# Attention, Fourier mix and feed-forward in one kernel: every buffer of a group named singly, and batch 0's sums in two equal parts

## The chip, the core and the metric

The kernel runs on one core of one Trainium2 chip (trn2). The core has a matrix engine (TensorE, "PE" in the profile; its weight loads are shown apart as "PEld"), VectorE ("DVE"), ScalarE ("ACT"), GpSimd ("POOL") and SyncE ("SP"), each with its own queue of instructions that run in the order in which they were written. Data lie in SBUF, matmul results in PSUM, which is split into eight banks. DMA transfers are issued by an engine's queue ("SPq", "POOLq", "ACTq") and run beside it.

The metric is the time on the device in microseconds (us), from runs of the whole kernel. The profile comes from one further execution.

## The reference

Inputs are q, k and v of shape (4, 8, 768, 64) (batch, heads, sequence, head dimension), and two weights of 512 x 2048 and 2048 x 512. All are fp32, as is the output of 4 x 768 x 512. Cut to what matters:

```python
scores = scale * q @ k.T                     # per batch and head, 768 x 768
keep   = (key < 8) | (0 <= query - key < 96) # 8 global keys, 96 local ones
scores = where(keep, scores - slope[h] * dist, -1e9)
a      = exp(scores - max); a = a / (sum(a) + 1e-9)
x      = concat_heads(a @ v)                 # 4 x 768 x 512
u      = x + real(fft(fft(x, axis=1), axis=2))
un     = (u - mean(u)) / sqrt(var(u) + 1e-6)
out    = u + relu(un @ w_ch1) @ w_ch2
```

## The kernel before

**Tiling.** Matmuls take fp16. The sequence has six blocks of 128 rows, the model dimension four of 128, the hidden layer sixteen. Heads go in pairs, so that a batch has four pairs, and pair n = 4b + hp carries its number through the names: `v_5` is the v of batch 1, pair 1. Attention computes only the band around the diagonal and the eight global keys. For a pair there are a cast of q and k to fp16, their transposes `qkT`, three score tiles `sc_n_g`, each followed by an exp on ACT (`ex`), and, once all pairs of a part are there, `pav` (probabilities times v), which VectorE divides by the row sums to give `x` (L762 reciprocal, L763 product; together "the norm"). In batches 0 and 1 the rows of v are also rearranged by matmuls with an identity (`v_place`: POOL casts the landed v at L437, the matmuls `pvp_n` follow at L453).

The Fourier mix of a batch starts with sums and differences of x on VectorE (`fold_s`, L810 to L829, then `fold_d`, L904 to L921), goes on with `py` matmuls (transform over the sequence, four groups), whose results ACT and DVE move to SBUF, and `pu` matmuls (over the model dimension; three pairs of row residues for each batch, so 12 units c = 3b + pr). An addition on VectorE (L1046, L1055) adds x back. For this addition x is needed with its rows in another order: the kernel writes x to DRAM (`xd`, L782, two halves of the columns for batch 0) and reads it back as `xr` (L790). Then come the statistics (`sm`, L1067), the scaling `un` (L1077, L1079, L1086), its transposes `ptu` and `unT`, the first feed-forward matmul `ph` in eight units for each c (L1144, relu at L1150 on ACT or L1151 on DVE) and the second, `pg` (L1167; for c of 8 and above the form of `pgA` and `pgD` at L1248, which takes seven products of sums of blocks for eight), and the store of `u` to the output.

**Order.** The order of all instructions is made while the kernel is built, by the class `Plan`. It is a list scheduler: it keeps a clock `t` per engine, a dictionary `tok` of the times at which results are there, a list of work that is ready for DVE, ACT, POOL and SP (`later`, `emit`), and four streams of matmul units (`run`): MIX and ATT, in which it may look ten units ahead, and PH and PG, which go in order. At each step it takes the unit that can start first by its own clocks. Costs are formulas (`act`, `dve`, `pool`, `mm_us`), and the landings of the early DMAs are a table written by hand:

```python
LAND = {("xw", 0, 0): 34.0, ("xw", 0, 1): 36.0, ("xr", 0): 41.0,
        ("ld", 4, 2): 47.7, ("ld", 5, 2): 53.4, ("ld", 6, 2): 58.9, ("ld", 7, 2): 64.7, ... }
```

Here `("ld", 4, 2)` is the landing of v_4, `xw` the write of x and `xr` its read. What the planner decides is only the order in each queue; the waits on the chip are those that the data, the buffers and the DMA semaphores need. The v loads of batch 1 (L388) are issued by SP and come behind the read of xr by an explicit token (`("xi",)`). The weights are eight DMAs of POOL (L1395, L1400), the loads of batches 2 and 3 wait behind a small DMA that needs the last weight (L1409, `hold`).

**Buffers.** The planner counts the free buffers of a group itself. In PSUM, group `xx` has two slots of two banks each, and `C` and `D` are two more such slots in the early part; their banks go later to `ph` and `pg`, two slots of one bank each. `rings` holds for each group a list of the times at which a slot comes free; `slot` takes the first of the list, whichever of the physical slots that was, and `bank` asks the pool for the next tile of the group's tag, which the pool hands out in rotation. In SBUF, `buf(tag, i, ...)` asks for buffer i of a group with `bufs=NBUF[tag]`, again handed out in rotation; the planner makes the user of number i wait for the token `("free", tag, i - NBUF[tag])`. Groups with more than one buffer are `hT` 3, `qk` 2, `qs` 3, `qkT` 4, `er` 2, `v0` 2, `u` 4, `un` 2 and `unT` 2.

**Sums of batch 0.** `fold_s` splits batch 0's columns in three parts, 0 to 256, 256 to 384 and 384 to 512. Each part is ten VectorE instructions (`f1` to `f4`) and waits for the x of its own columns; batch 0's norms come in the order of pairs 0 and 1 together, pair 2, pair 3. The folds of batch 0 have rank -1 in the planner, so that it lets them go up to 0.8 us ahead of other work. The parts have numbers of their own in the groups `eA` and `ww` (functions `IA`, `NA`, `IW`).

Of the kernel before, what the change touches and what calls it, by code (L numbers as in the profile page):

```python
# [9 lines left out]
FP16 = mybir.dt.float16  # L10
# [2 lines left out]
ALU = mybir.AluOpType  # L13

P = 128


class Plan:
# [73 lines left out]
    def emit(self, place):  # L92
        ready, (_, ways, needs, after, outs, uses, ring, lat, dma, then, _, nd) = self.ready.pop(place)
        if nd:
            ready = [max(r, self.lanes[nd - 1]) for r in ready]
        ends = [max(self.t[w[0]], r) + w[1] for w, r in zip(ways, ready)]
        i = int(np.argmin(ends))
        eng, _, fn = ways[i]
        fn()
        end = self.t[eng] = ends[i]  # L100
        if dma:
            q = "DMA2" if outs and outs[0][0] in ("xw", "xr") and outs[0][1] == 0 else "DMA"
            end = self.t[q] = max(self.t[q], end) + dma
        else:
            lat += self.LAT.get(eng, 0.0)
        for o in outs:
            self.tok[o] = max(end + lat, self.LAND.get(o, 0.0)) if dma else (end + lat, eng)
        for u in uses:
            self.used(u, end + lat)
        for _ in range(nd):  # L110
            self.lanes.append(max(end + lat, self.t[eng] + 2.2, *[self.LAND.get(o, 0.0) for o in outs]))
            self.lanes.pop(0)
        if ring is not None:
            self.rings[ring].append(end + lat)
        if then is not None:
            then(end + lat)
        self.promote()
# [8 lines left out]
        return end + 0.15  # L126

    def slot(self, tag):
        return self.rings[tag].pop(0)

    LOOK = 10
    AHEAD = 0.8
# [1 line left out]
    def run(self, streams):  # L134

        left = [list(s) for s, _ in streams]
        while True:
            best = None
            for i, s in enumerate(left):
                for k, (needs, ring, _) in enumerate(s[:self.LOOK if streams[i][1] else 1]):  # L140
                    if not self.known(needs):
                        continue
                    r = self.at(needs, "PE")
                    if ring is not None:

                        there = [(self.rings[g][0], g) for g in ring
                                 if self.rings[g] and not (g in ("C", "D") and ("CD",) in self.tok)]
                        if not there:
                            continue
                        t, g = min(there)  # L150
                        r = max(r, t + self.SEM)
                    else:
                        g = None
                    c = (max(r, self.t["PE"]), i, k, g or "")
                    if best is None or c < best:
                        best = c
            op = self.first()
            if op is not None and (best is None or op[0] <= best[0]):
                self.emit(op[4])
            elif best is not None:  # L160
                needs, ring, fn = left[best[1]].pop(best[2])
                if ring is not None:
                    self.slot(best[3])
                fn(best[0], best[3])
# [29 lines left out]
def kernel(  # L194
# [82 lines left out]

    pl = Plan()
    RING = {"xx": 2, "ph": 2, "pg": 2}
    pl.rings = {r: [0.0] * n for r, n in RING.items()}  # L280

    pl.rings["C"] = [0.0]
    pl.rings["D"] = [0.0]
# [4 lines left out]
    def bank(tag, name, dtype=FP32):  # L288
        if tag in ("C", "D"):
            return early["pool"].tile([P, 2, 512 if dtype == FP32 else 1024], dtype, tag=tag, name=name, bufs=1)  # L290
        if tag == "xx":
            return ps.tile([P, 2, 512 if dtype == FP32 else 1024], dtype, tag=tag, name=name, bufs=RING[tag])
        if "late" not in early:
            early["ctx"].__exit__(None, None, None)
            early["late"] = ctx.enter_context(tc.tile_pool(name="psl", bufs=1, space=bass.MemoryType.PSUM))
        return early["late"].tile([P, 512], FP32, tag=tag, name=name, bufs=RING[tag])


    NBUF = {"hT": 3, "qk": 2, "qs": 3, "qkT": 4, "er": 2, "v0": 2, "eg": 1, "x": 1, "xr": 1, "zy": 1, "eA": 1,
# [5 lines left out]

    def buf(tag, i, shape, dtype, users):
        pl.users(("free", tag, i), users)
        return wk.tile(shape, dtype, tag=tag, name=f"{tag}_{i}", bufs=NBUF[tag])

    ident = kon.tile([P, 256], FP16, tag="ident", name="ident")  # L310
    sel_sb = ident[:, 128:256]
# [129 lines left out]
    def v_place(b, hp):  # L441
        n = HP * b + hp

        def run(start, ring):
# [17 lines left out]
            def freed(t):  # L462
                done.append(t)
                if len(done) == 2:
                    pl.rings[ring].append(max(done))
                    for x in CD(b, ring):
                        pl.used(x, max(done))
            for a in range(2):
# [80 lines left out]
    def trans(b, hp):  # L549
        if b >= FB:  # L550
            return trans_dma(b, hp)
        n = HP * b + hp

        def run(start, ring):
            pt = bank("xx", f"pt_{n}", FP16)
# [161 lines left out]
    def av(b, part, jp):  # L717
# [8 lines left out]
        def run(start, ring):  # L726
# [30 lines left out]

            def norm():
                if b not in X:
                    X[b] = buf(XT[b][0], XT[b][1], [P, NS, Dm], FP16, 4 if b else 5)  # L760
                rc = wk.tile([P, 2, nh, 1], FP32, tag="rc", name=f"rc_{b}_{first}_{jp}", bufs=2)
                V.reciprocal(rc, pv[:, :, :, 64:65])  # L762
                VT(X[b][:, 2 * jp:2 * jp + 2, first * Dh:(first + nh) * Dh].rearrange("p j (h d) -> p j h d", d=Dh),  # L763
# [88 lines left out]
    def fold_3(b):  # L852

# [280 lines left out]
    def ph_unit(c, jp):  # L1134
        needs = [("unT", c), ("w1", jp // 2)] + (free("hT", 4 + c) if jp == 0 else []) + [("CD",)]

        def run(start, ring):
            if jp == 0:
                HT[c] = buf("hT", 4 + c, [P, NJ, CH], FP16, 2 if c < CS else 1)
            ph = bank("ph", f"ph_{c}_{jp}")  # L1140
            for a in range(2):
                jb = 2 * jp + a
                for d in range(ND):
# [13 lines left out]
    def pg_unit(c, t, part):  # L1157
# [3 lines left out]

        def run(start, ring):
            if part == 0:
                GP[0] = bank("pg", f"pg_{c}_{t}")
            pg = GP[0]
            for jb in range(4 * part, 4 * part + 4):
                nc.tensor.matmul(pg, HT[c][:, jb, t * P:(t + 1) * P], W2[0][:, jb, :],  # L1167
# [10 lines left out]
            pl.later([("DVE", dve(512), add)], [("rstd", c)], e, [("ob", i)], ring="pg", rank=0)  # L1178
# [62 lines left out]
    def pg_units(c):  # L1241
# [24 lines left out]
            V.scalar_tensor_tensor(o, x, r(t), acc, op0=ALU.mult, op1=ALU.add)  # L1266

        def p1(start, ring):
            A_ = GP[c, "A"] = bank("pg", f"pgA_{c}")
            prod(A_[:, 0:HC], a(0, 0), bw(0, 0), True)  # L1270
            e = pl.pe(one_us, start)
            pl.later([("DVE", dve(HC), lambda: stt(u(0)[:, 0:HC], A_[:, 0:HC], 0, u(0)[:, 0:HC]))],
                     [("rstd", c)], e, [("ra", c, 0)], rank=0)

        def p45(start, ring):
            D_ = GP[c, "D"] = bank("pg", f"pgD_{c}")
# [15 lines left out]
        def p32(start, ring):  # L1292
# [3 lines left out]
            e = pl.pe(2 * one_us, start)  # L1296
            pl.used(("free", "sx", 3 * (c - CS) + 2), e)
            pl.later([("DVE", dve(Dm), lambda: stt(u(0), D_, 0, u(0)))],
                     [("ra", c, 1)], e, [("ob", c, 0)], ring="pg", rank=0)

        def p7(start, ring):
            A_ = GP[c, "A"]
# [7 lines left out]
            pl.later([("DVE", dve(Dm), last)], [("rd", c, 0)], e, [("ob", c, 1)], ring="pg", rank=0)  # L1310

        h0 = [("h", c, jp) for jp in range(4)]
        h1 = [("h", c, jp) for jp in range(4, 8)]
# [15 lines left out]
    with tc.manual_schedule():  # L1329
# [9 lines left out]
            load(0, hp, "v")  # L1339

        V.memset(EG, 0.0)
        pz = bank("xx", "pz")
# [25 lines left out]

        def ones(start, ring):

            pv = bank("xx", "pones")
# [153 lines left out]
```

## Time and profile before

| what | value |
|---|---|
| time, median of 5 runs | 270.75 us (270.43 to 272.6) |
| time of the profiled execution | 270.43 us |
| its span, first to last instruction | 268.2 us |
| mean granted TensorE clock | 0.985 |
| matmuls `ph` (L1144) | 768, busy 94.3 us |
| matmuls `pg` (L1167) | 256, busy 60.2 us |
| matmuls `pav` (L743) | 352, busy 17.3 us |
| exps of scores on ACT (L629, L632) | 24 and 24, 0.94 and 0.93 us each |
| relu on ACT (L1150) / DVE (L1151) | 78 of 0.60 us / 18 of 0.69 us |
| loads of v (L388, of all batches) | 16 DMAs of 192 KB, 4.6 us from issue to landing |
| weight loads on POOL's queue | 8 DMAs of 512 KB, 17.1 us from issue to landing |

The first row is what a user of the kernel sees; the profile explains only the execution in the second row, and 2.2 us of it lie outside the span. Busy time is a sum over the whole span, and the mean of one instruction can mix shapes. The last two rows are medians of the time from the issue, most of which a transfer can spend waiting behind others. The page of the profile also gives the busy share of each engine in 40 slices of 6.7 us; TensorE and the granted clock (tenths of full speed) read:

```profile
PE   7898889689999999999999999999999999999993
PEclk9999799979999999999999999999999999999999
```

The low digit in the eighth slice (47 to 54 us) and the low clock in the ninth (54 to 60 us) lie in one stretch of the kernel, in which batch 1's attention and batch 0's Fourier mix run together. The clock is also low in the fifth slice (27 to 34 us).

### The profile page before, as it was taken

To read this page: it belongs to the slowest core of one execution; us is meant where nothing else is said; L and a number is where in the kernel's file an instruction comes from. 1 tells how busy PE (TensorE), PEld (TensorE's weight loads), DVE (VectorE), ACT (ScalarE), POOL (GpSimd) and SP (SyncE) were. 2 spreads that over 40 slices of the span, in tenths; PEclk is the share of its full clock that TensorE was granted. 3 is DMA by queue.
4 is the path that set the end of the run, shared out by engine and by line. 5 is a ranking of instruction groups with operands and counts; after the bars stand their busy time and mean duration, and the time that the engine had idled before them with its cause. 6 is when DMAs were issued, how large, how long until landed. Compare 5 with 4: busy or idle time off the path is not lost.

```text
span 268.2 us, 6166 instructions
## 1 busy us (share of the span) xinstructions
PE 254.0 (95%) x2512; PEld 181.7 (68%) x2512; DVE 175.8 (66%) x375; ACT 146.1 (54%) x244; POOL 67.3 (25%) x131
## 2 busy tenths in 40 slices
PE   7898889689999999999999999999999999999993
PEld 3444745468784696778776466778865678888882
DVE  4558796833169955863269968777999756536172
ACT  1479698667557254896590135897432245543400
POOL 1443187322211342344021417202000402010000
PEclk9999799979999999999999999999999999999999
DMA  7999969999559995968589795610055133402022
GB/s 205 290 292 282 293 122 248 217 216 216 132 103 216 270 293 111 224 154 154 119 198 206 185 279 126 162 34 7 4 123 192 39 93 27 117 2 78 2 78 78
DMA packets 75180, 41.50 MB, mean 155 GB/s; under 512 B 32402, under 2 KB 71314, under 8 KB 75154
## 3 DMA queue, kind: packets, MB, share of 16 engines
q1 hardware_dynamic: 68098, 32.22, 50.7%
q0 software_dynamic: 4224, 4.19, 9.7%
q10 hardware_dynamic: 2832, 4.72, 6.0%
q8 instruction: 19, 0.31, 0.5%
q14 instruction: 7, 0.06, 0.1%
HBM read 31.42 MB, written 9.44 MB: 152 GB/s over the span
## 4 chain that ended last, share of the span: by engine, by line
PE 71%; DMA 11%; SPq 5%; ACT 5%; DVE 5%; issue 1%; POOL 0%; ACTq 0%
PE ph L1144 31%; PE pg L1167 16%; DMA qs<-in_v_dram 7%; PE pgD L1248 5%; SPq L388 4%; PE pav L743 4%; PE pgA L1248 3%; PE pu L1027 3%; DMA w<-in_q_dram 3%; PE sc L607 3%; PE py L947 3%; ACT ex L632 2%; DMA out_dram<-u 2%; PE pav L732 1%; ACT qkT L571 1%
## 5 line engine op out<-in xcount | busy, mean ns | idle before, releaser
L1144 PE MATMUL ph<-unT,w 128*128 128x256 f16 x768 | 94.3, 275 | 0.1
L1144 PEld LDWEIGHTS <-w 128*128 128x128 f16 x768 | 73.6, 98 | 14.1 <-issue 3.0
L1150 ACT ACTIVATE hT<-ph 128x512 f16<-128x512 f32 x78 | 46.2, 598 | 49.1 <-PE ph L1144 44.1
L1167 PE MATMUL pg<-w,hT 128*128 128x512 f16 x256 | 60.2, 379 | 0.0
L1167 PEld LDWEIGHTS <-hT 128*128 128x128 f16 x256 | 24.2, 98 | 23.8 <-issue 0.2
L632 ACT ACTIVATE ex<-sc 128x992 f16<-128x992 f32 (+2 forms) x24 | 21.2, 932 | 7.0 <-PE sc L609 6.9
L629 ACT ACTIVATE er<-sc 128x992 f16<-128x992 f32 (+2 forms) x24 | 21.6, 938 | 3.2 <-PE sc L607 3.2
L644 DVE TENSOR_TENSOR ex<-er,mk 128x992 f16<-128x992 f16 (+2 forms) x24 | 16.1, 677 | 5.7 <-ACT er L629 5.6
L1151 DVE TENSOR_SCALAR hT<-ph 128x512 f16<-128x512 f32 x18 | 12.4, 688 | 10.1 <-PE ph L1144 10.0
L995 POOL COPY ww<-zy 128x512 f16<-128x512 f16 x16 | 9.6, 622 | 35.2 <-PE py L947 35.2
L743 PE MATMUL pav<-v,ex 128*128 128x65 f16 x352 | 17.3, 197 | 1.0 <-ACT ex L632 1.0
L743 PEld LDWEIGHTS <-ex 128*128 128x128 f16 x352 | 16.1, 100 | 2.4 <-issue 1.6
L1176 DVE SCALAR_TENSOR_TENSOR u<-pg,sm,u 128x512 f32<-128x512 f32 x16 | 12.0, 747 | 8.3 <-PE pg L1167 8.2
L1093 POOL TENSOR_SCALAR sm<-sm 128x2 f32<-128x2 f32 x12 | 3.0, 250 | 50.1 <-ACT un L1086 50.0
L1086 ACT ACTIVATE un<-un 128x512 f16<-128x512 f16 x24 | 15.1, 631 | 0.7 <-PE ptu L1116 0.5
L1046 DVE SCALAR_TENSOR_TENSOR u<-pu,xr 128x512 f32<-128x512 f32 x18 | 11.7, 687 | 4.3 <-PE pu L1027 4.3
L1248 PEld LDWEIGHTS <-hT 128*128 128x128 f16 x128 | 12.5, 98 | 2.7 <-issue 1.0
L396 POOL CAST qk<-qs 128x768 f16<-128x768 f32 x9 | 9.1, 1008 | 20.9 <-DMA qkT<-qk 9.4
L482 POOL CAST v<-qs 128x768 f16<-128x768 f32 x8 | 7.5, 940 | 27.0 <-DMA qs<-in_v_dram 26.9
L962 ACT ACTIVATE zy<-py 128x1024 f16<-128x1024 f32 (+1 forms) x10 | 8.3, 854 | 11.0 <-PE py L947 7.1
L1266 DVE SCALAR_TENSOR_TENSOR u<-pgD,sm,u 128x512 f32<-128x512 f32 x8 | 6.0, 750 | 11.3 <-PE pgD L1248 11.3
L763 DVE TENSOR_TENSOR x<-pav,rc 128x512 f16<-128x512 f32 (+1 forms) x21 | 12.9, 615 | 0.7
(124 smaller groups left out, 390.7 us busy)
## 6 DMA issues: line engine op xcount, KB each, us to landing
out_dram<-u SPq DMA_DIRECT2D x24, 256.0 KB, 2.2
w<-in_moe_w_ch_dram POOLq DMA_DIRECT2D x8, 512.0 KB, 17.1
qs<-in_q_dram SPq DMA_DIRECT2D x9, 384.0 KB, 4.7
qs<-in_k_dram SPq DMA_DIRECT2D x9, 384.0 KB, 4.6
qs<-in_v_dram SPq DMA_DIRECT2D x16, 192.0 KB, 4.6
xr<-xd ACTq DMA_DIRECT2D x3, 768.0 KB, 4.9
u<-in_v_dram SPq DMA_DIRECT2D x5, 384.0 KB, 6.8
w<-in_q_dram SPq DMA_DIRECT2D x4, 384.0 KB, 7.1
```

The costliest lines, as they stand in the source:

```text
L629: A(mine(), cut(pa), AF.Exp, 0.0, 0.125)
L632: A(cut(expst[hp][:, :, g * 512:g * 512 + (384 if g == 2 else 512)]), cut(pa), AF.Exp, 0.0, 0.125)
L644: VT(o, mine(), m, op=ALU.mult)
L743: nc.tensor.matmul(po[:, jj, hh * 65:(hh + 1) * 65], lhsT, v16[b % 2][:, i, h, 0:65], start=(jp == 0 and a == 0), stop=(a == len(ops) - 1) ...
L763: VT(X[b][:, 2 * jp:2 * jp + 2, first * Dh:(first + nh) * Dh].rearrange("p j (h d) -> p j h d", d=Dh), pv[:, :, :, 0:Dh], rc.to_broadcast( ...
L1086: A(x, x, AF.Square, accum_out=MV[c][:, a, 2:3])
L1144: nc.tensor.matmul(ph[:, a * CH:(a + 1) * CH].rearrange("p (x m) -> p x m", x=2), W1[0][:, d, jb * P:(jb + 1) * P], UNT[c][:, :, d, :], st ...
L1150: pl.later([("ACT", act(512), lambda: A(dst, ph, AF.Relu)), ("DVE", dve(512), lambda: V.tensor_scalar_max(dst, ph, 0.0))], [], e, [("h", c ...
L1151: ("DVE", dve(512), lambda: V.tensor_scalar_max(dst, ph, 0.0))],
L1167: nc.tensor.matmul(pg, HT[c][:, jb, t * P:(t + 1) * P], W2[0][:, jb, :], start=(jb == 0), stop=(jb == NJ - 1))
L1176: V.scalar_tensor_tensor(UT[c][:, t, :], pg, MV[c][:, t, 3:4], UT[c][:, t, :], op0=ALU.mult, op1=ALU.add)
L1248: nc.tensor.matmul(o, lhs(j), rhs(j), start=(first and j == 0), stop=(j == NK - 1), skip_group_check=True)
```

## The change

The change has two parts.

1. **Naming.** A slot of a PSUM group now carries its number: the planner's list holds pairs of time and number, `slot` takes the pair with the smallest time (the slot that has been free longest) and returns a `Ring`, a string with the number `k`. `bank` builds a tag from group and number, with one buffer each, so that the physical slot is the one that the planner chose. In SBUF, the tag is built from the group and `i % NBUF`, again with one buffer each, so that buffer i takes the place of buffer i - NBUF. The functions that give a slot back (`later(ring=...)`) pass the ring they were given, which for `pg` means keeping it in `GP`.
2. **Sums.** Batch 0's columns are folded in two parts of 256. The counts of users and the numbers of the parts in `eA` and `ww` follow from that. Both halves of the columns now need all norms of their two pairs, so the second part waits for the norms of pairs 2 and 3.

The code of the second part is one line and its counts. The planner builds the whole order anew, so other instructions change places too; they are named in the prediction where they matter.

```diff
+class Ring(str):
+
+    k = 0
...
         if ring is not None:
-            self.rings[ring].append(end + lat)
+            self.rings[ring].append((end + lat, ring.k))
...
     def slot(self, tag):
-        return self.rings[tag].pop(0)
+        tag = Ring(tag)
+        t = min(self.rings[tag])
+        self.rings[tag].remove(t)
+        tag.k = t[1]
+        return tag
...
-                        there = [(self.rings[g][0], g) for g in ring
+                        there = [(min(self.rings[g])[0], g) for g in ring
...
-    pl.rings = {r: [0.0] * n for r, n in RING.items()}
+    pl.rings = {r: [(0.0, k) for k in range(n)] for r, n in RING.items()}
...
         if tag == "xx":
-            return ps.tile([P, 2, 512 if dtype == FP32 else 1024], dtype, tag=tag, name=name, bufs=RING[tag])
+            return ps.tile([P, 2, 512 if dtype == FP32 else 1024], dtype, tag=f"{tag}{tag.k}", name=name, bufs=1)
...
-        return early["late"].tile([P, 512], FP32, tag=tag, name=name, bufs=RING[tag])
+        return early["late"].tile([P, 512], FP32, tag=f"{tag}{tag.k}", name=name, bufs=1)
...
-        return wk.tile(shape, dtype, tag=tag, name=f"{tag}_{i}", bufs=NBUF[tag])
+        return wk.tile(shape, dtype, tag=f"{tag}_{i % NBUF[tag]}", name=f"{tag}_{i}", bufs=1)
...
-                    X[b] = buf(XT[b][0], XT[b][1], [P, NS, Dm], FP16, 4 if b else 5)
+                    X[b] = buf(XT[b][0], XT[b][1], [P, NS, Dm], FP16, 4)
...
-        parts = ((0, 256), (256, 128), (384, 128)) if b == 0 else ((0, 512),)
+        parts = ((0, 256), (256, 256)) if b == 0 else ((0, 512),)
...
-        return n if b == 0 else 2 + 2 * b + n
+        return n if b == 0 else 1 + 2 * b + n
...
-        return 1 if b else 3
+        return 1 if b else 2
...
-        return n if b == 0 else 2 + 3 * b + n
+        return n if b == 0 else 1 + 3 * b + n
...
-                GP[0] = bank("pg", f"pg_{c}_{t}")
+                GP[0] = bank(ring, f"pg_{c}_{t}")
+                GP[1] = ring
```

More of the change, by code (lines that the diff above doesn't have):

```diff
@@ L161, in run @@
                 needs, ring, fn = left[best[1]].pop(best[2])
-                if ring is not None:
-                    self.slot(best[3])
-                fn(best[0], best[3])
+                fn(best[0], self.slot(best[3]) if ring is not None else "")
                 self.promote()
@@ L279 @@
     RING = {"xx": 2, "ph": 2, "pg": 2}
-    pl.rings = {r: [0.0] * n for r, n in RING.items()}
-    pl.rings["C"] = [0.0]
-    pl.rings["D"] = [0.0]
+    pl.rings = {r: [(0.0, k) for k in range(n)] for r, n in RING.items()}
+    pl.rings["C"] = [(0.0, 0)]
+    pl.rings["D"] = [(0.0, 0)]
     early = {"ctx": tc.tile_pool(name="pse", bufs=1, space=bass.MemoryType.PSUM)}
@@ L464, in freed @@
                 if len(done) == 2:
-                    pl.rings[ring].append(max(done))
+                    pl.rings[ring].append((max(done), ring.k))
                     for x in CD(b, ring):
@@ L554, in run @@
         def run(start, ring):
-            pt = bank("xx", f"pt_{n}", FP16)
+            pt = bank(ring, f"pt_{n}", FP16)
             src = qk16.pop(n)
@@ L1139, in run @@
                 HT[c] = buf("hT", 4 + c, [P, NJ, CH], FP16, 2 if c < CS else 1)
-            ph = bank("ph", f"ph_{c}_{jp}")
+            ph = bank(ring, f"ph_{c}_{jp}")
             for a in range(2):
@@ L1177, in add @@
                                        op0=ALU.mult, op1=ALU.add)
-            pl.later([("DVE", dve(512), add)], [("rstd", c)], e, [("ob", i)], ring="pg", rank=0)
+            pl.later([("DVE", dve(512), add)], [("rstd", c)], e, [("ob", i)], ring=GP[1], rank=0)
             def st():
@@ L1268, in p1 @@
         def p1(start, ring):
-            A_ = GP[c, "A"] = bank("pg", f"pgA_{c}")
+            A_ = GP[c, "A"] = bank(ring, f"pgA_{c}")
+            GP[c, "Ar"] = ring
             prod(A_[:, 0:HC], a(0, 0), bw(0, 0), True)
@@ L1275, in p45 @@
         def p45(start, ring):
-            D_ = GP[c, "D"] = bank("pg", f"pgD_{c}")
+            D_ = GP[c, "D"] = bank(ring, f"pgD_{c}")
+            GP[c, "Dr"] = ring
             prod(D_[:, 0:HC], a(1, 1), tw(2), True)
@@ L1298, in p32 @@
             pl.later([("DVE", dve(Dm), lambda: stt(u(0), D_, 0, u(0)))],
-                     [("ra", c, 1)], e, [("ob", c, 0)], ring="pg", rank=0)
+                     [("ra", c, 1)], e, [("ob", c, 0)], ring=GP[c, "Dr"], rank=0)
         def p7(start, ring):
@@ L1309, in last @@
                 stt(o, A_[:, 0:HC].unsqueeze(1).to_broadcast([P, 2, HC]), 1, o)
-            pl.later([("DVE", dve(Dm), last)], [("rd", c, 0)], e, [("ob", c, 1)], ring="pg", rank=0)
+            pl.later([("DVE", dve(Dm), last)], [("rd", c, 0)], e, [("ob", c, 1)], ring=GP[c, "Ar"], rank=0)
         h0 = [("h", c, jp) for jp in range(4)]
@@ L1341 @@
         V.memset(EG, 0.0)
-        pz = bank("xx", "pz")
+        z = Ring("xx")
+        z.k = 1
+        pz = bank(z, "pz")
         for _ in range(12):
@@ L1369, in ones @@
         def ones(start, ring):
-            pv = bank("xx", "pones")
+            pv = bank(ring, "pones")
             for half in range(2):
```

## The prediction

> **What bounds the kernel now.** I read the busy times first, then TensorE's idle times in order of time, then the chain of waits, and last what VectorE and the two DMA queues did just before the largest wait. TensorE (PE) is busy for 95% of the span, so a gain must come from its idle time or from a slow clock.
>
> ```profile
> PE 254.0 (95%) x2512; PEld 181.7 (68%) x2512; DVE 175.8 (66%) x375; ACT 146.1 (54%) x244; POOL 67.3 (25%) x131
> 40.00:50.00 10.00, 9.45 (x97) 5.68 (x96) 7.18 (x17) 8.43 (x14) 7.39 (x15) 1.00 1.16 238
> 50.00:60.00 10.00, 6.71 (x79) 4.93 (x77) 5.21 (x15) 6.48 (x16) 2.10 (x4) 0.83 1.19 215
> 60.00:70.00 10.00, 10.00 (x108) 8.29 (x106) 3.22 (x6) 6.91 (x16) 3.36 (x7) 1.00 1.05 188
> ```
>
> In the table by stretches (PE is the first busy figure, the granted clock the third from the end) the hole is at 50 to 60 us: 6.71 of 10, at a clock of 0.83. From 60 us to about 215 us PE is full. TensorE in order of time shows what ends the hole, and the chain of waits what stands behind it:
>
> ```profile
> 50.05 1.06 PE L1027 MATMUL pu<-t,ww 128*128 128x128 f16 x16
> 53.99 0.36 PE L453 MATMUL pvp<-v,ident 64*64 64x128 f16 x12 [2.88 <-POOL v L437]
> ...
> 59.42 0.36 PE L453 MATMUL pvp<-v,ident 64*64 64x128 f16 x12 [0.41 <-POOL v L437]
> 40.05 18.44 DMA qs<-in_v_dram
> 58.54 0.84 POOL v L437
> 59.42 0.36 PE pvp L453 x12
> ```
>
> PE stands for batch 1's v, cast by POOL as it lands. The v loads are issued by SP behind the read xr of batch 0 (L790), which waits for the second pair of writes xd (L782), which wait for the last norms of attention (L762, L763). VectorE and SP there:
>
> ```profile
> 31.60 0.42 DVE L763 TENSOR_TENSOR x<-pav,rc 128x256 f16<-128x256 f32 x1
> 32.06 0.36 DVE L810 TENSOR_TENSOR eA<-x 128x384 f16<-128x384 f16 x1
> ...
> 33.81 0.28 DVE L829 SCALAR_TENSOR_TENSOR zy<-ww,eA 128x128 f16<-128x128 f16 x1
> 34.02 0.17 DVE L762 RECIPROCAL rc<-pav 128x4 f32<-128x4 f32 x1
> ...
> 34.77 0.42 DVE L763 TENSOR_TENSOR x<-pav,rc 128x256 f16<-128x256 f32 x1
> 35.23 0.64 DVE L810 TENSOR_TENSOR eA<-x 128x384 f16<-128x384 f16 x1
> 35.79 0.97 DVE L811 TENSOR_TENSOR eA<-x 128x384 f16<-128x384 f16 x1
> 39.07 0.35 SPq L790 DMA_DIRECT2D xr<-xd  x1
> 39.47 7.57 SPq L388 DMA_DIRECT2D qs<-in_v_dram  x3
> ```
>
> The sums of columns 256 to 384 (ten instructions, 32.06 to 34.09) stand in front of the last two norms, whose matmuls were done by about 32.1.
>
> **Part 1: two equal parts.** The three-part split leaves the DVE queue ten 128-wide instructions in the way; now the last two norms come first. They took 34.02 to 35.19, 1.17 us, so they end at 32.06 + 1.17 = 33.2: **2.0 us earlier**. The xd pair was issued at 35.23 and 35.84 and landed at 38.92; it lands at 36.9, and xr and the v loads behind it are issued 2.0 us earlier, xr at 37.05. One 256-wide part took 23.76 to 26.93, so sums end about 33.2 + 3.1 + 0.9 = 37.2 instead of 38.2. The 0.9 is what L810 and L811 above lost against 0.36 and 0.35 beside POOL's casts at 34.83 to 36.5. On that the Trainium skill ("SBUF — State Buffer", section "SBUF: two separate sides") speaks against the change: a VectorE operation with two SBUF inputs and a GpSimd operation lock each other out for a whole instruction. Two casts of 0.86 would then cost up to 1.7 and end the sums at 38.0. Either is covered: the first y matmuls also need ACT's evictions and cannot start before about 39.9.
>
> What 2.0 us at the issue are worth at the landing is the main unknown. The trace's packets: the weight loads of POOL (issued from 36.50) move from 38.2, xr (issued 39.07) from 43.24, and it lands at 47.2; then v at 53.06, 58.49, 63.88 and 69.59, one per 5.4 to 5.9 us because 1 KB packets of weights and 512 B packets of v alternate. SP's queue moved almost nothing between 34.6 and 36.5 and after 38.9. The Trainium skill ("DMA: Bandwidth & Descriptors", section "Queues, rings and completion order") says that each DMA engine takes turns between queues, packet by packet. By that rule an xr issued as the weights start is served from about 39; its 128 packets of 6 KB took 43.24 to 46.8 in company, 3.6 us less the tail, so it lands near 42 to 43, **4 to 5 us earlier**, and all four v with it. By the row, xr waited 4.2 us behind weights already queued: then data start at 41.2 and it lands 2 to 3 us earlier. I take the nearer half of the rule (3.5 to 5), since at 37.05 only one weight load is queued ahead, not two and part of a third. The ends are 2.0 and 5.
>
> PE's side, with durations from the trace (score 0.83, 0.82, 0.69; pu 0.89; ptu 0.45; ph 0.87; pvp 0.29). Up to py_0_1 ACT is full (32.84 to 46) and its qkT eviction still ends at 42.05, so nothing moves. Then py_0_1, py_0_2, sc_6_1, pu_0, sc_6_2, sc_7_0 to 7_2, pu_1, pu_2, ptu_0 in the new order give 42.05 + 0.87 + 0.66 + 0.82 + 0.89 + 0.69 + 0.83 + 0.82 + 0.69 + 0.89 + 0.89 + 0.45 = 50.6 for pvp_4, with the ACT evictions between (about 0.85 each) just in front of each. In this order ACT's exp of sc_7_0 stands behind the small sm_0, which waits for pu_0's add and so for xr: harmless up to a landing near 46. After pvp_4 the second half of un_1 stands on ACT behind pvp_4's eviction; ptu_1 is late by about 0.65 and ph_0_0 starts near 52.8 instead of 54.99. With ph_0_1, ph_0_2 and ptu_2 before it, pvp_5 can run at 55.95 and that state ends at 56.25. Before, the same set of work (through ph_0_2) ended at 61.05: **4.8 us**. This presumes full clock; the half-rate window 55.47 to 58.88 cost 0.38 on ph_0_0 and 0.41 on ptu_1, and may come again. The next v caps it: pvp_6 ran at 65.0 and can run 0.9 after its landing, 59.8 to 61.9 for shifts of 5 to 3; PE is there at 60.1. So early gain 3.1 to 4.8, **4.2** taken.
>
> The weights lose about 1 us to the earlier xr. The first was in at 43.6 and is needed at 52.8; the last at 70.3, needed near 74. The loads of batch 2 wait for that last one (L1409) and don't move earlier.
>
> **Part 2: buffers named singly.** In PSUM the write takes the oldest free bank instead of the one the rotation gives. The wait of sc_4_1 for qkT (0.8 us at 33.5) goes, but ACT is full behind it: zero. In SBUF the loads of batch 2 wait for the casts that free their own buffer: 79.22 becomes about 75.5, 85.41 about 78.7. PE does not wait for them before (qkT of the first pair landed at 104.08, its scores ran at 110.5) and should not after (needed near 106.6). ACT's 5.0 us stop before 92 us (L790, behind an output store that shares its semaphore) shrinks: 0.24 at ph_2_1.
>
> **Part 3: the order that the planner makes of it.** The wait of pgD_8 at 218.8 (0.68 with its lead-in) goes, as ph_9_0 and ph_9_1 now stand between the last pg_7_1 and pgA_8, and two more pg groups behind the last ph remove some 0.4 at 257 to 263. Against it, between 105 and 122 us PE meets the scores of batch 2 earlier: 13.0 us of PE work beside 13.1 of ACT work, where ACT was busy 9.12 of 10. I allow 1.0 us of new stalls, between 0 and 2. Sum: 4.2 + 0.24 + 0.68 + 0.4 - 1.0 = **4.5 us**.
>
> The profiled execution took 270.43 us for a span of 268.2; the median of the runs is 270.75. So the span becomes 263.7 and the time 270.43 - 4.5 = 265.9; with the 0.3 by which the median lies above this execution, 266.2.
>
> **Rivals.**
> - *The v stream moves by only 2 us* (xr keeps its place behind the weights). For: the 4.2 us before its first packet. Against: the idle SP queue. pvp_6 at 62.9 gives 2.1, the rest adds 0.3: 268.3.
> - *No change.* The hole fills with another wait, such as un_1 behind pvp_4 on ACT plus a second half-rate window (up to 1.7 us) and 2 us of ACT stalls: about 270.3. Against it, each is bounded by rows above.
> - *Slower: ACT becomes the bound.* PE pulled ahead runs into the exps of batches 2 and 3 before ACT can serve them: 105 to 122 us (ACT 9.12 of 10) and 170 to 185 (ACT 5.00 of 5 in each of three stretches). Each score tile holds one of two banks until its exp of 0.93 us is done. If ACT falls back by one exp per pair of heads, eight in all, that is 7.4 us against 5.5 gained: 272.6. It decides from six such exps on. Against: after 60 us PE had next to no stall before, with the same ACT work in all.
> - *The naming does nothing* (the rotation already gave the oldest bank) is contained in the first sum, where part 2 is worth 0.24.
>
> **Chances.** Forecast 0.54 (265 to 267.5), v stream by 2 us 0.27, no change 0.08, slower 0.10, faster than 264.5 0.01. Half a per cent, 1.35 us, is about what a measurement of this kernel can tell from no change: faster by more 0.81, within 0.08, slower 0.11. The range 264.3 to 269.8 takes in the shifts of 2 to 5 us and 0 to 2 us of new stalls, and leaves out about 0.19.
>
> **What would show it.** Right: the last x norm near 33 us, xr issued near 37 and landing before 44, v landing near 48 to 50, the pvp wait for POOL under 1 us, PE over 8.5 of 10 between 50 and 60. Wrong: xr landing at 45 or later; PE waiting for ACT after sc between 105 and 185; the first ph after 54 us.

## The result and the profile after

| kernel | median | runs | ratio to before (95% interval) |
|---|---|---|---|
| before | 270.4 us | 269.31 to 272.6 | |
| after | 267.99 us | 266.53 to 269.75 | 0.9918 (0.9901 to 0.9935) |

The change makes the kernel 0.8% faster, 2.2 us by the ratio (0.0082 x 270.4). The forecast was 4.5 us. Ratios, here and below, are estimated without the runs that lie more than 1.5% above the fastest of their kernel, while medians and ranges take in every run (it concerns three of twelve runs of the sums alone and one of a later kernel), so that a ratio need not be the quotient of two medians. The profiled execution after took 269.28 us for a span of 267.5, so it is 1.3 us slower than the median of its kernel; before, it took 270.43 and 268.2.

The page's busy line after and the table by stretches (columns as before: PE is the first busy figure, the granted clock the third from the end):

```profile
PE 252.3 (94%) x2512; PEld 179.0 (67%) x2512; DVE 176.7 (66%) x364; ACT 148.5 (56%) x248; POOL 63.1 (24%) x128
...
50.00:60.00 10.00, 8.57 (x114) 7.00 (x111) 6.06 (x15) 7.76 (x21) 2.77 (x6) 1.00 1.20 216
60.00:70.00 10.00, 9.00 (x93) 6.86 (x91) 2.83 (x5) 5.57 (x13) 2.53 (x4) 1.00 0.95 166
```

From 50 to 60 us PE is busy 8.57 of 10 instead of 6.71, at full clock instead of 0.83. But from 60 to 70 us it loses 1.0, where it had lost nothing. TensorE in order of time:

```profile
50.44 0.36 PE L460 MATMUL pvp<-v,ident 64*64 64x128 f16 x12
...
56.78 0.36 PE L460 MATMUL pvp<-v,ident 64*64 64x128 f16 x12 [0.76 <-POOL v L444]
...
62.11 0.36 PE L460 MATMUL pvp<-v,ident 64*64 64x128 f16 x12 [1.00 <-POOL v L444]
```

The 2.88 us that PE stood for v_4 are gone. It now stands for v_5 and v_6. On VectorE, the norms go first, and the second sums follow at once:

```profile
32.34 0.42 DVE L770 TENSOR_TENSOR x<-pav,rc 128x256 f16<-128x256 f32 x1
...
34.54 0.91 DVE L828 TENSOR_TENSOR zy<-eA,ww 128x256 f16<-128x256 f16 x1
35.38 0.90 DVE L829 TENSOR_TENSOR zy<-eA,ww 128x256 f16<-128x256 f16 x1
```

The landings in the two traces:

| | before | after |
|---|---|---|
| last x norm ends | 35.19 | 32.76 |
| xr issued, landed | 39.07, 47.20 | 37.09, 43.85 |
| v_4, v_5, v_6, v_7 landed | 53.06, 58.49, 63.88, 69.59 | 49.25, 55.85, 61.12, 66.64 |
| pvp_6 on PE | 65.00 | 62.11 |
| last matmul's group (pgA_11) starts | 262.94 | 262.29 |

At v_6 the new kernel is **2.9 us ahead; at the end 0.65**. So 2.2 us were given back between 65 us and the end. The trace after shows three places, each of which had no such stall before: 0.67 us in pu_5 (95 us), 1.27 us between ptu_6 and pu_8 (166 us), 0.56 us in pu_11 (210 us). (Two of these are counted at the weight loads, the middle one from the usual time of ptu_6; by the matmuls' modelled ends they are 0.50, 1.11 and 0.39.) Two of them:

```profile
92.74 0.82 POOL L489 CAST v<-qs 128x768 f16<-128x768 f32 x1
93.51 1.72 POOL L1002 COPY ww<-zy 128x512 f16<-128x512 f16 x3
...
95.29 0.95 PE L1034 MATMUL pu<-t,ww 128*128 128x128 f16 x14 [0.50 <-POOL ww L1002]
...
166.93 1.02 ACT L1131 ACTIVATE unT<-ptu 128x1024 f16<-128x1024 f16 x1 [1.16 <-PE ptu L1123]
...
168.01 1.05 PE L1034 MATMUL pu<-t,ww 128*128 128x128 f16 x16 [1.11 <-ACT unT L1131]
```

At 92.74 POOL casts a landed v of batch 2 ahead of the mirror copies that pu_5 needs. At 166 us the unit pu_8 comes two units after pu_7 and finds both `xx` slots in use, one with ptu_6 until ACT has moved it.

### The profile page after: what moved, and what is told of

Same layout as the page of the kernel before. It is cut to its first block, busy times and chain, and to the rows that moved or that the text cites. A ratio compares the mean times of both kernels' runs of the same rounds, so it can differ in the third digit from the quotient of the medians.

```text
span 267.5 us, 6159 instructions
## 1 busy us (share of the span) xinstructions
PE 252.3 (94%) x2512; PEld 179.0 (67%) x2512; DVE 176.7 (66%) x364; ACT 148.5 (56%) x248; POOL 63.1 (24%) x128
## 3 DMA queue, kind: packets, MB, share of 16 engines
q0 software_dynamic: 4224, 4.19, 9.4%
## 4 chain that ended last, share of the span: by engine, by line
PE 70%; DMA 11%; DVE 5%; POOL 5%; ACT 3%; issue 2%; SPq 1%; POOLq 0%; DVEq 0%
PE ph L1151 29%; PE pg L1175 16%; DMA qs<-in_v_dram 8%; PE pgD L1256 5%; PE pgA L1256 4%; PE pav L750 3%; PE py L954 3%; DMA u<-in_v_dram 3%; PE sc L614 3%; PE pu L1034 2%; POOL ww L1002 2%; ACT ex L639 2%; PE pav L739 1%; SPq L395 1%; ACT qk L399 1%
## 5 line engine op out<-in xcount | busy, mean ns | idle before, releaser
L1151 PE MATMUL ph<-unT,w 128*128 128x256 f16 x768 | 93.4, 273 | 0.2 <-ACT eg L715 0.2
L1157 ACT ACTIVATE hT<-ph 128x512 f16<-128x512 f32 x76 | 45.2, 597 | 51.7 <-PE ph L1151 50.5
L1158 DVE TENSOR_SCALAR hT<-ph 128x512 f16<-128x512 f32 x20 | 13.8, 689 | 9.2 <-PE ph L1151 9.0
L750 PE MATMUL pav<-v,ex 128*128 128x65 f16 x352 | 16.4, 193 | 0.9 <-ACT ex L639 0.9
L750 PEld LDWEIGHTS <-ex 128*128 128x128 f16 x352 | 15.1, 97 | 2.5 <-issue 1.5
L399 ACT ACTIVATE qk<-qs 128x768 f16<-128x768 f32 x12 | 10.0, 844 | 8.4 <-DMA xd<-x 4.6
L1274 DVE SCALAR_TENSOR_TENSOR u<-pgA,sm,u 128x256 f32<-128x256 f32 (+1 forms) x12 | 6.9, 572 | 9.9 <-PE pgA L1256 9.5
L489 POOL CAST v<-qs 128x768 f16<-128x768 f32 x8 | 6.6, 827 | 28.2 <-DMA qs<-in_v_dram 28.1
```

The source lines that it names most:

```text
L750: nc.tensor.matmul(po[:, jj, hh * 65:(hh + 1) * 65], lhsT, v16[b % 2][:, i, h, 0:65], start=(jp == 0 and a == 0), stop=(a == len(ops) - 1) ...
L1151: nc.tensor.matmul(ph[:, a * CH:(a + 1) * CH].rearrange("p (x m) -> p x m", x=2), W1[0][:, d, jb * P:(jb + 1) * P], UNT[c][:, :, d, :], st ...
L1157: pl.later([("ACT", act(512), lambda: A(dst, ph, AF.Relu)), ("DVE", dve(512), lambda: V.tensor_scalar_max(dst, ph, 0.0))], [], e, [("h", c ...
L1158: ("DVE", dve(512), lambda: V.tensor_scalar_max(dst, ph, 0.0))],
```

## The experiments

Three questions: which part of the change makes the gain, why the v loads moved by less than forecast, and whether they can be had earlier. Times are medians; the ratio is always to the kernel before, run beside it on the same chip.

**The two parts singly.** First the sums alone, put into the kernel before:

```diff
-        parts = ((0, 256), (256, 128), (384, 128)) if b == 0 else ((0, 512),)
+        parts = ((0, 256), (256, 256)) if b == 0 else ((0, 512),)
```

> The kernel before with only the sums of batch 0 in two parts; buffers by rotation as before. My theory (the gain comes from the last norms going ahead of the second sums, so that xr and with it v land earlier): the last x norm ends near 33 us, xr lands near 44, v_4 near 49, and nearly all of the 2.2 us is there: ratio to before 0.990 to 0.993. Rival (the gain comes from the buffers and the order that the planner makes with them): ratio 0.998 or more, though v lands earlier.

Measured (`a_two_parts`): 271.67 us (268.59 to 274.13), ratio 1.0024 (0.9990 to 1.0057). xr landed at 43.62 and v_6 at 61.04 as in the change, but nothing is gained in the median, and the spread is 5.5 us. Then the change with the three parts put back (the reverse of this diff):

> The changed kernel with three parts again, so the naming alone. My theory: xr and v land as before (47 and 53 us), PE waits about 3 us for v_4 as before, ratio to before 0.997 to 1.001. Rival (naming and its order make the gain): ratio 0.994 or less.

Measured (`b_naming_three`): 270.75 us, ratio 1.0028 (1.0005 to 1.0052); v_4 landed at 52.93, PE stood 2.75 us for it. **Neither part alone gains; together they gain 0.8%.** My theory, that it is all in the sums, fell.

**The naming alone, at one order.** Here the changed planner makes the order, and only the physical buffers are handed out in rotation again, so that every engine runs the same instructions in the same order:

```diff
-        return wk.tile(shape, dtype, tag=f"{tag}_{i % NBUF[tag]}", name=f"{tag}_{i}", bufs=1)
+        return wk.tile(shape, dtype, tag=tag, name=f"{tag}_{i}", bufs=NBUF[tag])
-            return ps.tile([P, 2, 512 if dtype == FP32 else 1024], dtype, tag=f"{tag}{tag.k}", name=name, bufs=1)
+            return ps.tile([P, 2, 512 if dtype == FP32 else 1024], dtype, tag=str(tag), name=name, bufs=RING[tag])
-        return early["late"].tile([P, 512], FP32, tag=f"{tag}{tag.k}", name=name, bufs=1)
+        return early["late"].tile([P, 512], FP32, tag=str(tag), name=name, bufs=RING[tag])
```

> The changed kernel with every instruction in the same order on every engine, but the buffers handed out in rotation again, in SBUF and PSUM. Shows what the naming does to the waits alone. My theory: within 0.5 us of the changed kernel, ratio to before 0.990 to 0.994, since what the oldest free buffer saves lies beside full engines. Rival (the naming's own waits carry the gain): ratio over 0.997, with new PE idle times behind PSUM evictions or loads of batch 2 landing over 3 us later.

Measured (`c_rot_both`): 269.10 us, ratio 0.9965 (0.9942 to 0.9988): about 1.3 us lost against the change (0.9965 - 0.9918). Between both theories. So each half by itself:

> The changed kernel, same order on every engine, with rotation put back in SBUF alone. With rotation in both the ratio to before was 0.9965 against 0.9918, so the naming's waits are worth some 1.3 us. My theory now: it is SBUF (the read xr of batch 1 was issued at 89.25 instead of 85.01 us and ACT stood before it): ratio 0.9955 to 0.9975, xr of batch 1 again at 88 us or later. Rival (it is PSUM): ratio 0.991 to 0.993.

Measured (`c_rot_sbuf`): 269.26 us, ratio 0.9955 (0.9932 to 0.9978). The read xr of batch 1 was issued at 88.14 us instead of 85.01, and in a `py` unit of batch 1 PE stood for ACT, where the change has no such wait:

```profile
90.83 0.60 PE L954 MATMUL py<-t,eA 128*128 128x256 f16 x4 [1.54 <-ACT zy L969]
```

> The changed kernel, same order on every engine, with rotation put back in PSUM alone. My theory (SBUF carries it): ratio 0.991 to 0.993, xr of batch 1 issued near 85 us. Rival (PSUM carries it): ratio 0.9955 to 0.9975.

Measured (`c_rot_psum`): 267.33 us, ratio 0.9889 (0.9852 to 0.9926); that read was issued at 83.81. The two traces can be compared directly: in both pvp_6 ran at 60.35, and from there to the last group of matmuls (261.62 and 259.85) rotation in SBUF costs 1.77 us, most of it the 1.54 us above. **The naming is worth its price in SBUF; in PSUM it shows no gain.**

**What the rotation costs the two parts.** The profile of the two-part kernel was of its fastest execution. A second profile:

> The kernel before with only the sums in two parts, a second look at an execution, since its times spread from 268.6 to 274.1 us and the profile was of the fastest. My theory: the executions differ behind 80 us, where with rotation the read xr of batch 1 and the loads of batch 2 wait for other buffers' users; in one that takes 271 us or more, PE shows 2 to 4 us more idle time between 85 and 170 us than in the first profile, and v_6 lands at 61 us as there. Rival: they differ before 65 us, v_6 landing 2 us or more later than 61 us.

Measured (`a_two_again`): 273.57 us, v_6 at 61.03 and pvp_6 within 0.02 us of the first profile, and then PE 5.0 us later by 122 us, more than the 2 to 4 expected. The granted clock was 1.00 throughout the kernel's work, so the clock is not the reason. The queues of SyncE and ACT and then PE in order of time in this execution, and after them one stretch of 2 us (the last figure is what the DMA engines moved, GB/s):

```profile
78.36 0.37 SPq L388 DMA_DIRECT2D qs<-in_q_dram  x1
...
85.52 0.38 SPq L388 DMA_DIRECT2D qs<-in_k_dram  x1
...
89.41 0.84 ACT L392 ACTIVATE qk<-qs 128x768 f16<-128x768 f32 x1 [4.22 <-DMA qs<-in_k_dram]
89.49 0.41 ACTq L790 DMA_DIRECT2D xr<-xd  x1
...
103.33 0.27 PE L1027 MATMUL pu<-t,zy 128*128 128x128 f16 x2 [2.10 <-DVE u L1046]
```

```profile
96.00:98.00 2.00, 2.00 (x28) 1.88 (x26) 0.00 (x0) 0.80 (x2) 0.56 (x2) 1.00 0.81 79
```

By rotation, the q load of pair 9 gets the buffer in which v of pair 8 lies, and waits for POOL's cast of it, to 78.33 us. The k load waits for POOL's cast of that q, to 85.49. (In the first profile it was issued at 82.81: q landed 1.1 us earlier, and the cast took 0.83 us instead of 2.42. Why it took longer here was not tested.) The cast of k stands on ACT at 89.41, and behind that on ACT stands the read xr of batch 1. It takes 12.35 us to land (8.74 in the first profile, 6.21 in the change). Its packets of 6 KB move from 92 to 101 us together with packets of 256 B, which from 95 us on, when the loads ahead of them in SyncE's queue had landed, can only be those of its two DMA transposes (landed at 101.70 and 102.09); all of them together move 112 GB/s from 94 to 96 us and 79 in the next two. In the change two transposes were issued beside the read too (84.54 and 86.91), but 123 of its 128 packets moved between 88 and 90 us, with 8% of the bytes from others and at 410 GB/s together. So the read is slow where its packets meet those of the transposes; why they meet in one execution and not in the other, and why they then move so slowly, stays open. The additions on VectorE wait for the read, and PE for their bank. The PE of the two profiles differs only behind 80 us: my theory held. If so, naming SBUF's buffers in the two-part kernel must give the gain, with the planner of before and rotation in PSUM:

```diff
-        return wk.tile(shape, dtype, tag=tag, name=f"{tag}_{i}", bufs=NBUF[tag])
+        return wk.tile(shape, dtype, tag=f"{tag}_{i % NBUF[tag]}", name=f"{tag}_{i}", bufs=1)
```

> The two-part kernel of a_two_parts, same order on every engine, with only SBUF's buffers named singly. My theory (the gain of the two parts is there before 65 us and is lost again near 90 to 120 us, where with rotation the loads of batch 2 wait for other buffers' users and the read xr of batch 1 is issued late and runs into DMA transposes): the spread of 268.6 to 274 us goes, xr of batch 1 is issued by 86 us and lands by 92, ratio to before 0.988 to 0.993. Rival (the order of the planner with the rings is what a_two_parts lacks): ratio 0.998 or more, spread as before.

Measured (`i_two_sbuf_named`): 267.26 us (266.69 to 268.07), ratio 0.9884 (0.9855 to 0.9913). The q and k loads were issued at 73.66 and 75.87, xr of batch 1 at 84.30 (its landing is not in the trace; the first addition that reads it ran at 93.4):

```profile
73.66 0.37 SPq L388 DMA_DIRECT2D qs<-in_q_dram  x1
...
75.87 0.41 SPq L388 DMA_DIRECT2D qs<-in_k_dram  x1
...
84.30 0.36 ACTq L790 DMA_DIRECT2D xr<-xd  x1
```

One line does it, at one order of instructions: 1.4% between the two kernels. So the two-part sums and the naming in SBUF are enough for the whole gain; neither the naming in PSUM nor the order that the changed planner makes is needed. Not all of the 1.4% need come from the later loads: in this profile xr's issue ended 0.2 us ahead of the first weight's, and pvp_6 ran at 60.88 instead of 62.04 in the first profile with rotation. Whether the naming or chance made that order is not shown.

**Does the early xd carry the gain?** In the change, six additions stand in front of the last two norms:

```diff
+                if b == 0 and first == 6 and jp == 1:
+                    for _ in range(6):
+                        VT(fill, dist_sb[:, 0:384], dist_sb[:, 0:384], op=ALU.add)
```

> The changed kernel, same order on every engine, with six additions of 384 columns into an unused tile (about 2.1 us of VectorE) put ahead of batch 0's last two norms, so that the second xd pair is issued as late as before while the order of PE stays the new one. My theory (the earlier xd is worth about what PE gains before 65 us): xr lands near 46 to 47, v_4 near 52 to 53, the pvp of v_5 and v_6 come 2 to 3 us later, and 2 to 3 us are lost: ratio to before 0.999 to 1.003. Rival (the new PE order, not the landing, makes the gain): under 0.7 us lost, ratio 0.992 to 0.995.

Measured (`f_filler`): 270.77 us, ratio 1.0038 (1.0016 to 1.0060). The additions took 2.31 us, xr landed at 46.13, v_6 at 62.43. PE stood for VectorE and then for v:

```profile
33.93 0.58 PE L601 MATMUL sc<-dist,sid 128*128 128x480 f16 x2 [1.75 <-DVE x L774]
...
53.06 0.36 PE L461 MATMUL pvp<-v,ident 64*64 64x128 f16 x12 [1.50 <-POOL v L445]
```

The whole gain and more is lost, so the early norms and what follows from them are needed, and the new order without them gains nothing. How much of the loss of 3.2 us (1.0038 - 0.9918) is the landing's own is less clear. The additions also hold VectorE and PE, by 1.75 us at 33.93; PE made that up, since it still had to stand 1.50 us for v_4. But v_6 landed only 1.3 us later than in the profile after and still 1.4 us earlier than before, and from profile to profile only 0.8 us are lost at the last group of matmuls. The profile after was of a slow execution of its kernel, that of the additions of the fastest of its own.

**The queue in front of xr.** In the next four kernels the planner still counts each weight load at its old place, and only the issue is put off, so that no other engine's order changes. First, the w2 loads behind POOL's cast of v_5 (in `cast_v0`):

```diff
+            if n == 5:
+                for i in held:
+                    wload(i)
...
-        pl.later([("POOL", 0.85, lambda i=i: wload(i))], needs, 0.0,
+        pl.later([("POOL", 0.85, lambda i=i: wload(i) if i < 4 else held.append(i))], needs, 0.0,
```

> The changed kernel, same order on every engine, but the four loads of w2 are issued by POOL behind its cast of v_5 instead of in front of it, so that v_5, v_6 and v_7 share the DMA engines with fewer weights. My theory (the v stream sets the end of this stretch; the waits of 0.76 and 1.00 us for v_5 and v_6 are its price): v_5 lands by 54 and v_6 by 58 us, both waits go, w2_0 lands before it is needed at 64 us, and 1.2 to 1.8 us are gained: ratio to before 0.985 to 0.988. Rival (PE meets the next wait, at ACT or at w2, or v's pace is set by its own queue): v_6 still lands after 60 us or pg waits for w2; ratio 0.990 to 0.994 or worse.

Measured (`e_w2_after_v5`): 268.44 us, ratio 0.9932 (0.9897 to 0.9967). v_6 landed at 56.40, 4.7 us earlier, and yet pvp_6 ran at 61.05: POOL spent 55.07 to 58.03 on the four issues and then took its small operations, and cast v_6 at 60.18:

```profile
55.07 2.96 POOL L1416 DMA_DIRECT2D w<-in_moe_w_ch_dram  x4
...
60.18 0.82 POOL L445 CAST v<-qs 128x768 f16<-128x768 f32 x1
```

So the wait moved from the DMA to POOL, and the gain that I had expected did not come: the ratio can't be told from that of the change. Next, the second weight load behind xr (in `kg_copies`; `held_w(n)` issues the next n loads put off):

```diff
+                if (n, s) == (6, 0):
+                    held_w(1)
```

> The changed kernel with one edit: POOL issues the second w1 load behind its first kG copy of pair 6 (about 37.7 us) instead of in front of it (36.5 to 37.0), so that xr is queued before it. My theory (xr waits for the weights that are already queued, so what counts is how many stand before it): xr lands at 40.5 to 42 us instead of 43.85, v_6 near 59.5 instead of 61.1, ratio to before 0.986 to 0.990. Rival (the DMA engines take turns, so one load more or less ahead does not matter): xr lands after 43 us, ratio 0.990 to 0.993.

Measured (`g_xr_first`): 267.59 us, ratio 0.9906 (0.9873 to 0.9939), which doesn't tell the theories apart; the trace does: xr landed at 43.28, v_6 at 60.77. xr was hardly helped, against my theory that the number of loads in front of it counts; the first weight load still stood before it. Both edits together, with w2 spread over the casts of v_5, v_6 and v_7:

> g_xr_first, and the w2 loads are issued by POOL one behind the cast of v_5, one behind v_6 and two behind v_7, so that v_6 and v_7 come in before w2 and POOL is not held for 3 us ahead of the cast of v_6. My theory: v_6 lands by 57 us, the wait of PE for it goes, nothing waits for w2: 0.3 to 1 us under g_xr_first, ratio 0.983 to 0.988. Rival (POOL's cast of v_6 stands behind small operations that need ACT, or pg now waits for w2): no gain over g_xr_first or a loss, ratio 0.988 to 0.995.

Measured (`h_xr_w2`): 272.47 us, ratio 1.0065 (1.0031 to 1.0100). v_6 landed at 56.35 and PE's wait for it went, as expected; but the last w2 landed at 73.43 instead of 69.13, the loads of batch 2 wait for it (`hold`), and PE then stood 4.2 us for an eviction (a move of results from PSUM to SBUF) that ACT reached late. Neither theory had named that. PE's wait in this kernel:

```profile
92.84 0.60 PE L963 MATMUL py<-t,eA 128*128 128x256 f16 x4 [4.19 <-ACT zy L978]
```

Last, the two first weight loads behind xr (`held_w(2)`), w2 untouched:

> The changed kernel with the first two w1 loads issued by POOL behind its first kG copy of pair 6 (about 37.6 us), so that xr (issued near 36.8) is queued before every weight. In g_xr_first only the second load was moved and xr still landed at 43.3, behind the first. My theory (the transfer queued first is served first; over the profiles xr took 4.3 us from issue to landing where its issue ended 0.2 us before the first weight's, 5.8 to 6.2 where it ended 0.2 to 0.3 behind, 6.6 to 7.7 where 0.4 to 0.7 behind, 8.1 where two weights were ahead): xr lands by 41.3 us, v_6 near 59.3, the w1 loads about 1 us later without a wait, the last w2 as before near 69.2, ratio to before 0.986 to 0.990 in a narrow spread. Rival (two loads moved back by 1 to 2 us end the stream of weights later, and batch 2's loads with it): last w2 after 70.5 us, ratio 0.991 or more.

Measured (`k_w_behind_xr`): **266.88 us (266.27 to 267.72), ratio 0.9882 (0.9854 to 0.9910)**. xr landed at 40.97, v_4 to v_7 at 42.34, 46.54, 51.95 and 57.40, the last w2 at 67.84. v_4 to v_7 came earlier than my theory had it (v_6 near 59.3), since xr and v_4 were in before the weights had moved much. The interval overlaps that of the change (0.9901 to 0.9935), so that this kernel beats the change is likely from its trace and its narrow range, but not clear of the noise. PE there, in the table by stretches and in order of time, with no wait for v left:

```profile
50.00:60.00 10.00, 9.33 (x125) 7.45 (x119) 5.82 (x13) 8.07 (x22) 2.98 (x5) 1.00 1.22 212
```

```profile
59.63 0.36 PE L460 MATMUL pvp<-v,ident 64*64 64x128 f16 x12
```

The DMA queues between 37 and 41 us show why (packets, MB, share of the engines), first in the change, then in this kernel:

```profile
q0 software_dynamic: 416, 0.43, 73.1%
q1 hardware_dynamic: 24, 0.15, 9.5%
```

```profile
q1 hardware_dynamic: 681, 1.06, 77.9%
```

q0 carries the weights, q1 xr and v. In the change xr was issued at 37.09, 1.0 us behind the first weight load, and had 24 of its 128 packets by 41 us; its first moved at 40.56. Here xr was issued at 36.50 and its first packet moved at 37.58; the weights, issued at 37.64, moved first at 41.77.

## Why the forecast was right in its direction and too large

The gain is clear of the noise and about half of the forecast. By the forecast's own sum nearly all of it, 4.2 of 4.5 us, was the sums' and 0.24 the naming's; measured, the sums alone gained nothing (1.0024), and they gain only with SBUF's naming. That the change as a whole went the forecast way is in part luck: without the naming, the same reasoning would have promised some 4 us and been wrong. The measured 267.99 us lie near the 268.3 of the rival "the v stream moves by only 2 us", and that is chance too: v moved by more than 2 us, PE gained 2.9, and 2.2 were lost again. The signs that I had named came nearly all as for a right forecast (last norm 32.76, xr landed 43.85, v_4 at 49.25, PE 8.57 of 10), since they tell of the stretch before 65 us and not at what is kept of it.

1. **xd earlier by 2.0 us: right.** The last norm came 2.4 us earlier, xr was issued at 37.09 (forecast 37.05). The sums ended at 37.2 as forecast, but by two errors that cancel: the norms were done 0.4 us sooner, and the two additions beside POOL's casts took 0.91 and 0.90 us against 0.28 to 0.29 without one, a loss of 1.2 us. I had put it at 0.9, and at 1.7 at the most.
2. **What that is worth at the landing: mis-sized.** I took 3.5 to 5 us for all four v, "the nearer half of the rule" of the Trainium skill ("DMA: Bandwidth & Descriptors", section "Queues, rings and completion order"), because only one weight load would be ahead. xr gained 3.35, v_4 3.8, but v_5 to v_7 only 2.6 to 3.0 (v_5 landed 6.6 us behind v_4 instead of 5.4; why is not shown). The row was the better guide: turns are taken packet by packet once both queues move (25 and 25 packets in each half microsecond at 42 us), but in these profiles the queue that comes second moves nothing for 2.1 to 3.8 us after the end of its issue, against 0.6 to 0.7 for xr where its issue ended first. Over the profiles, against the end of the first weight's issue:

| kernel | xr's issue ends | xr's first packet | issue to landing |
|---|---|---|---|
| i_two_sbuf_named, c_rot_psum | 0.2 us before | 37.7, 37.8 | 4.4, 4.3 |
| c_rot_sbuf, e_w2_after_v5, h_xr_w2 | 0.2, 0.3, 0.3 us behind | 38.8, 39.2, 39.1 | 5.8, 6.2, 6.1 |
| after | 0.4 us behind | 40.6 | 6.8 |
| a_two_parts, a_two_again, g_xr_first | 0.5, 0.7, 0.6 us behind | 40.3, 40.5, 40.1 | 7.1, 6.9, 6.6 |
| c_rot_both | 0.6 us behind | 40.9 | 7.7 |
| before, b_naming_three, f_filler | 2.0, 2.8, 2.7 us behind | 43.2, 43.4, 42.1 | 8.1, 7.9, 7.6 |

3. **PE's order and durations: right.** Forecast 50.6 for pvp_4 and 52.8 for the first ph, measured 50.44 and 52.75, at full clock. From there the v landings decided, and the term "4.2 taken" was 2.9. That 4.8 and more was to be had, k_w_behind_xr shows: pvp_6 at 59.63, 5.4 us earlier than before. (Two slips of the forecast change nothing: by its own 0.9 us behind a landing, pvp_6 could run at 59.8 to 61.8, not 61.9, and the first packet of a weight moved at 38.35, not 38.2.)
4. **Part 2 at 0.24: the mechanism right, the size wrong.** I had named the loads of batch 2 and ACT's stop before 92 us, and the loads moved as forecast (79.22 and 85.41 became 76.09 and 77.95; forecast 75.5 and 78.7). But I priced them by what PE lost in the kernel before. There PE came late and the stop was covered. With PE 3 us ahead the cover is gone, at least in part of the executions: rotation costs 1.3 us in the change's order and 3.8 in the two-part kernel (0.9884 against 1.0024), some of which may lie ahead of v_6, as said above. The gains of the parts don't add up.
5. **New stalls of 1.0 us between 105 and 122 us: wrong place and size.** There, hardly anything was added. The 2.5 us of pu_5, ptu_6 and pu_11 stood elsewhere, where the planner's order met POOL's queue and the two `xx` slots. I had costed ACT alone. Of the stalls that were to go, the one at pgA_8 (0.68) and the one at 92 us (0.24) went, the 0.4 at the end did not.

Sum of the profiles: 2.9 gained by v_6; then 0.24 + 0.68 gained, 2.5 lost, and some 0.7 in pieces of 0.1 to 0.3; 0.65 us of PE time are left. The runs show more, 2.2 us by the ratio and 2.4 by the medians. That the profiled execution was one of the slower ones of its kernel is measured; that the order of xr and the first weight in the queues decides between its executions is likely from the table, but no second execution of the change was profiled.

## What to carry to other kernels

Price a wait that is now covered by what it costs when the engine comes earlier, before adding gains up: here each part alone gave nothing. Look at which physical buffer a pool will hand out: a rotation that does not match the order of release makes one load wait for another tensor's reader, and everything behind it in that queue too. Where a small critical transfer and a bulk stream start within a microsecond of each other on two queues, fix their order by hand: here 0.6 us in the order of two issues (0.2 ahead to 0.4 behind) was 2.4 us from issue to landing.

## What the runs showed that was not expected

- The late start of the second queue holds both ways: in k_w_behind_xr the weights came second, and their first packet moved 3.2 us after the end of their issue (38.58 to 41.77); in the kernel before it was xr, 3.8 us.
- A read of 6 KB packets together with DMA transposes was slow: 79 to 112 GB/s between 94 and 98 us in the second profile of the two-part kernel, against 216 GB/s from 50 to 60 us in the change.
- The half-rate stretch of 55.47 to 58.88 us, whose return the forecast had named as possible (0.38 and 0.41 us), did not come in the execution after: the granted clock was 1.00 there. Behind 40 us three profiles show such a stretch ahead of the kernel's end, each 3.41 us long and each begun within 1.5 us of a long wait of PE: before (2.88 us), b_naming_three (2.75) and h_xr_w2 (4.19). Waits of up to 2.10 us (a_two_again at 103.33) had none behind them. Nothing here was run to test what sets it.
